# Block 0 of X in four transposing loads of 128 columns, with the Wq quarters between them

## The chip, the cores and the metric

The kernel runs on one core of one Trainium2 chip. The time is device microseconds of one execution; three runs of the kernel before have a median of 168.35 us (168.29 to 169.01). Profiles are taken in an execution of their own; their times count from the first instruction of the span.

The core's engines each run their own instruction queue: PE (matrix products; PEld is its weight load), DVE (VectorE), ACT (ScalarE), POOL (GpSimd) and SP, which only issues DMAs here. They wait for each other on semaphores.

## The reference

Two mixers share the input row-wise through a gate. With S = 2048 rows and D = 512 columns, bfloat16:

```python
x = A_x
g = sigmoid((x * gate_w).sum(-1))
a = sliding_dilated_attention(x, wqkv) @ wo    # 32 heads of 16, 8 keys at distance 0, 2, .., 14
h = layernorm(x)
u = gelu(einsum("bsd,sf->bdf", h, w1) + b1)    # F = 1792
b = (einsum("bdf,fs->bds", u, w2) + b2)        # transposed back to (S, D)
out = g * a + (1 - g) * b
```

The attention first needs q, k and v, three products of x (2048 x 512) with a 512 x 512 part of wqkv each. The change touches the loads for the first of these products.

## The kernel before, in words

The kernel is built from a list of operations, each with its engine, an estimated duration and the buffers it reads and writes. A planner (the class `_Sched`) derives the dependences, orders the operations of every engine greedily by an estimated start and the length of the work that follows, and then plans the waits. For DMAs an estimated landing time can be written by hand (`lands`). Explicit chains at the end fix the order of DVE almost wholly and that of ACT in part; PE's and the rest of ACT's order come out of the planner, so an edited estimate can reorder them.

X is needed in two layouts. Plain X (16 tiles of 128 rows) serves layernorm; XT, its transpose, with 4 tiles of 128 columns (index `dt`) by 2048 rows, is the moving operand of the projections. XT is loaded by transposing DMAs, in four blocks of 512 rows (`sb`). A projection of one block for one group `dl` sums over the four column tiles: four matmuls of 128 x 128 by 512, a weight tile of WQKV each.

In order of time:

- PE first runs warm-up matmuls on constants (L525: nine of 512 columns and one of 256), which are not used.
- Block 0 of q and k goes through eight PSUM banks at once (L609 to L614, matmuls at L593). For q the loop goes over the column tiles outermost: the four groups with column tile 0 (one matmul each), then with tile 1, and so on. Then k, with two column tiles at a time. Here the matmul with column tile `dt` needs that quarter of Wq and, in the kernel before, the whole block 0 of XT.
- The other blocks and v follow (L623 to L632). ACT evicts each group to SBUF (L601 for q, L604 for k and v).
- DVE computes statistics of plain X for layernorm (L548), and products of q with shifted k (L663). PE sums these over a head's columns in two bursts (`qkr_0` and `qkr_1`, L671), which ACT evicts (L701). The second pass of L663 writes over buffers that the first burst reads.
- Softmax on DVE and ACT (L711 to L750), with exponentials at L736; then DVE's weighted sums of v (L770 to L775).
- Meanwhile PE runs the first product of the token mixer (L785), four matmuls per quarter of the rows and 16 per group, each group into one of four banks, evicted by gelu on ACT (L806), and then the second (L835, evicted at L903). At the end come the product with wo (L851), its gated sum on DVE (L872), and the output's DMAs.

The loads issue on SP in the order they are listed in `first_loads` and after it; SP handles one issue at a time, and a wait or a long issue holds everything behind it. The first quarter of Wq issues from ACT's queue (it is named `act` in the list). Issues after the first eight wait for an earlier load (`throttle`: five back in `init_dmas`). L467 is the transposing load of block 0, L460 that of the other blocks, L429 every plain load.

Of the kernel before, what the change touches and what calls it, by code (L numbers as in the profile page):

```python
# [13 lines left out]
D = 512  # L14
# [4 lines left out]
NST = S // 128  # L19
# [314 lines left out]
def bass_gated_mix__sliding_local_dilated__mixer_token_mlp__prompt_kernel(nc, A_x, A_wqkv, A_wo, B_x, B_w1, B_b1, B_w2, B_b2, gate_w, out, dbg=None):  # L334
    with contextlib.ExitStack() as es:
# [3 lines left out]
        sch = _Sched()  # L339

        x2d = A_x[0]
# [7 lines left out]
        XT = view("XT", BF16, [(S, 4), (1, S)])  # L349
# [65 lines left out]
        A = sch.add  # L415
# [12 lines left out]
        def mk_dma(dst, src):  # L428
            return lambda e: e.dma_start(dst, src)  # L429

        init_dmas = []

        def throttle():
            return [init_dmas[-5]] if len(init_dmas) >= 5 else []

        def prev_dma():
            return [init_dmas[-1]] if init_dmas else []

        def ld_x(t0, n, q="sp"):
            ds = sch.dsem("x%d" % t0)  # L440
            op = sch.dma(q, mk_dma(X[:, t0:t0 + n, :], xv[:, t0:t0 + n, :]), n * 128 * D * 2, ds,
                         writes=["x%d" % t for t in range(t0, t0 + n)], deps=throttle() if q == "sp" else [], after=prev_dma() if q == "sp" else [], name="d_x%d" % t0)
            if q == "sp":
                init_dmas.append(op)
            return op

        def ld_w(tn, d0, n, q="sp"):
            ds = sch.dsem("wqkv%d_%d" % (tn, d0))
            op = sch.dma(q, mk_dma(WQKV[:, d0:d0 + n, tn * D:(tn + 1) * D], wqkv_v[:, d0:d0 + n, tn * D:(tn + 1) * D]),
                         n * 128 * D * 2, ds, writes=["wqkv%d_%d" % (tn, dt) for dt in range(d0, d0 + n)],  # L450
                         deps=throttle() if q == "sp" and n == 4 else [], after=prev_dma() if q == "sp" else [],
                         issue=0.65 if n == 4 else 0.45, name="d_wp%d_%d" % (tn, d0))
            if q == "sp":
                init_dmas.append(op)
            return op

        def ld_xt(sb):
            ds = sch.dsem("xt%d" % sb)
            dst = XT[:, :, sb * 512:(sb + 1) * 512]
            op = sch.dma("sp", lambda e: e.dma_start_transpose(dst, x2d[sb * 512:(sb + 1) * 512, :]), 512 * D * 2, ds,  # L460
                         writes=["xt_%d" % t for t in range(4 * sb, 4 * sb + 4)], deps=throttle(), after=prev_dma(), name="d_xt%d" % sb)
            init_dmas.append(op)

        def ld_xt0(s0, s1):
            ds = sch.dsem("xt0_%d" % s0)
            dst = XT[:, :, s0:s1]
            op = sch.dma("sp", lambda e: e.dma_start_transpose(dst, x2d[s0:s1, :]), (s1 - s0) * D * 2, ds, issue=1.25,  # L467
                         writes=["xt_%d" % t for t in range(s0 // 128, s1 // 128)], after=prev_dma(), name="d_xt0_%d" % s0)
            init_dmas.append(op)
            return op  # L470

        first_loads = [ld_w(0, 0, 1, "act"), ld_xt0(0, 512), ld_w(0, 1, 1), ld_w(0, 2, 1), ld_w(0, 3, 1), ld_w(1, 0, 2), ld_w(1, 2, 2),
                       ld_x(0, 2)]
        ld_xt(1)
        first_loads.append(init_dmas[-1])
        for op_, t_ in zip(first_loads, (2.9, 4.9, 5.4, 5.8, 6.2, 7.0, 7.8, 8.6, 11.0)):
            op_.lands = t_
            op_.deps.clear()
        init_dmas[:] = [first_loads[1]] + first_loads[5:]
        ld_x(2, 2)  # L480
        ld_x(4, 4)
        ld_xt(2)
# [6 lines left out]
        def ld_w1(j):  # L489
# [4 lines left out]
            if j < 4:  # L494
# [8 lines left out]
                       writes=["wo"], deps=throttle(), after=prev_dma(), name="d_wo")  # L503
# [4 lines left out]
        for i_, (v_, n_) in enumerate(((B_b1, NFT), (B_b2, NST))):  # L508
            vr = v_.rearrange("(t q j) -> q t j", q=4, j=32)
            for q_ in range(4):  # L510
                sch.dma("sp", mk_dma(psub(BR, 32 * q_, n_, 32 * i_, [(1, 32)]), vr[q_]), n_ * 64, ds_b, reads=["br"],
                        writes=["br_%d_%d" % (i_, q_)], deps=throttle(), after=prev_dma(), name="d_b_%d_%d" % (i_, q_), issue=0.45)
        d_w1.append(ld_w1(3))
        A("dve", lambda e: e.transpose(out=BT, in_=BR), 0.2, reads=["br_%d_%d" % (i_, q_) for i_ in range(2) for q_ in range(4)],
          writes=["btc"], name="t_b")
# [5 lines left out]
        def f_warm(n, w_=D):  # L521
            def fn(e):
                ins = None
                for _ in range(n):
                    ins = e.matmul(ps[:, 7, 0:w_], lhsT=CONE[:, 0:128], rhs=CONE[:, 0:w_], start=True, stop=True)  # L525
                return ins
            return fn

        A("pe", f_warm(9), 3.84, writes=["lg7_0", "lg7_1"], name="warm1", prio=-100)
        last_tx = A("pe", f_warm(1, 256), 0.2, writes=["lg7_0", "lg7_1"], name="warm2", prio=-100)  # L530

        ALLXT = ["xt_%d" % t for t in range(NST)]

        JK = view("OUTS", BF16, [(1, D)], extra=0)
        def cols(v_, lo, n, step=1):
# [9 lines left out]
        for hf in range(2):  # L545
            t0 = 8 * hf
            for t in range(t0, t0 + 8):
                A("dve", (lambda t_: (lambda e: e.bn_stats(out=ST6[:, t_, :], in_=X[:, t_, :])))(t), 0.59,  # L548
                  reads=["x%d" % t], writes=["st6_%d" % t], name="ln1_%d" % t, prio=0)
# [13 lines left out]
              reads=["zc%d" % hf], writes=["sd%d" % hf], name="ln_sqrt%d" % hf, prio=0)  # L563
            A("dve", (lambda t0_: (lambda e: e.reciprocal(out=cols(RSTD, t0_, 8), in_=cols(SD, t0_, 8))))(t0), 0.25,
              reads=["sd%d" % hf], writes=["rstd%d" % hf], name="ln_rstd%d" % hf, prio=0)
# [17 lines left out]
        def main_bank():  # L583
            b = main_idx[0] % 4
            main_idx[0] += 1
            return b
# [22 lines left out]
        for (b0, d0, d1, s0, s1) in ((0, 0, 1, 0, 512), (0, 1, 2, 0, 512), (0, 2, 3, 0, 512), (0, 3, 4, 0, 512), (4, 0, 2, 0, 512), (4, 2, 4, 0, 512)):  # L609
            for b in range(b0, b0 + 4):  # L610
                tn, dl = first[b]
                last_main[0] = A("pe", f_proj(tn, dl, 0, b, d0, d1, s0, s1), 0.216 * (d1 - d0) * (s1 - s0) / 512,
                                 reads=ALLXT[s0 // 128:s1 // 128] + ["wqkv%d_%d" % (tn, dt) for dt in range(d0, d1)],
                                 writes=fbn[b], after=[last_main[0]], name="pf_%s%d_%d_%d" % (tnames[tn], dl, d0, s0))  # L614
        for b, (tn, dl) in enumerate(first):
            A("act", f_evq(tn, dl, 0, b), 0.52, reads=fbn[b] + (["k5pad"] if tn == 1 else []),
              writes=["%s5_%d_0" % (tnames[tn], dl)], name="ev_%s%d_0" % (tnames[tn], dl), prio=0)
# [5 lines left out]
        for dl in range(4):  # L623
            seq_proj += [(2, dl, sb) for sb in range(4)]
        for (tn, dl, sb) in seq_proj:
            xr = ALLXT[4 * sb:4 * sb + 4]
            bank = main_bank()
            last_main[0] = A("pe", f_proj(tn, dl, sb, bank), 0.866,
                             reads=xr + ["wqkv%d_%d" % (tn, dt) for dt in range(4)],
                             writes=["acc%d" % bank], after=[last_main[0]], name="pj_%s%d_%d" % (tnames[tn], dl, sb), prio=0)  # L630
            A("act", f_evq(tn, dl, sb, bank), 0.62, reads=["acc%d" % bank] + (["k5pad"] if tn == 1 else ["v5pad"] if tn == 2 else []),
              writes=["%s5_%d_%d" % (tnames[tn], dl, sb)], name="ev_%s%d_%d" % (tnames[tn], dl, sb), prio=0)  # L632
# [11 lines left out]
                writes=["xa"] + ["wqkv%d_%d" % (tn, dt) for tn in range(3) for dt in range(4)], name="d_xa")  # L644
        for t in range(NST):
# [5 lines left out]
          writes=["th"], name="g_tanh", prio=0)  # L651
        A("dve", lambda e: e.tensor_scalar(out=G, in0=TH, scalar1=0.5, scalar2=0.5, op0=ALU.mult, op1=ALU.add), 0.15,
          reads=["th"], writes=["g"], name="g_g", prio=0)
        A("dve", lambda e: e.tensor_scalar(out=OMG, in0=TH, scalar1=-0.5, scalar2=0.5, op0=ALU.mult, op1=ALU.add), 0.15,
          reads=["th"], writes=["omg"], name="g_omg", prio=0)
        A("dve", lambda e: e.tensor_tensor(out=C2, in0=OMG, in1=B2C, op=ALU.mult), 0.15,
          reads=["omg", "b2c"], writes=["c2"], name="g_c2", prio=0)
# [25 lines left out]
        for wh in range(2):  # L683
# [6 lines left out]
            for (dl, c0, nc_) in pieces:  # L690
# [3 lines left out]
                  reads=["q5_%d_%d" % (dl, sb) for sb in range(c0, c0 + nc_)] +  # L694
                        ["k5_%d_%d" % (dl, sb) for sb in range(max(c0 - 1, 0), c0 + nc_)] + ["k5pad"],
                  writes=wr, name="qkm_%d_%d_%d" % (wh, dl, c0), prio=0)
            rd = sum([pbn(b_) for b_ in bufs], []) + PBX[wh] + ["rp"]
            for wl in range(4):
                qop = A("pe", f_qkr(list(enumerate(bufs)), (wl,)), 0.92, reads=rd, writes=["lg%d_0" % (4 + wl), "lg%d_1" % (4 + wl)],
                        name="qkr_%d_%d" % (wh, wl), prio=-100 + wl, delay=BURST_DELAY)  # L700
                A("act", (lambda wh_, wl_: (lambda e: e.activation(out=ATT[:, :, 4 * wh_ + wl_, :], in_=ps[:, 4 + wl_, :].rearrange("p (h c) -> p h c", h=2), func=AF.Copy)))(wh, wl),  # L701
                  0.55, reads=["lg%d_0" % (4 + wl), "lg%d_1" % (4 + wl)], writes=["lw%d" % (4 * wh + wl)],
                  name="lev_%d_%d" % (wh, wl), prio=0)
# [24 lines left out]
        for hf in range(2):  # L728
# [3 lines left out]
              reads=["outs1"], writes=["lh%d" % hf] + (wall if hf == 0 else []), name="sm_sub%d" % hf, prio=0)  # L732
            if hf == 0:
                A("act", lambda e: e.activation(out=col(SD, 0), in_=col(ZC, 0), func=AF.Exp, scale=0.0), 1.5,
                  reads=["zc0"], writes=["sd0"], name="sm_pre")
            A("act", (lambda hf_, l_: (lambda e: e.activation(out=ATT[:, hf_], in_=l_, func=AF.Exp)))(hf, lgh), 1.95,  # L736
              reads=["lh%d" % hf], writes=["att%d" % hf], name="sm_exp%d" % hf, prio=0)
        for hf in range(2):
# [5 lines left out]
            def f_rcp(e, hf_=hf):  # L744
# [6 lines left out]
              reads=["rs%d" % hf], writes=["att%d" % hf], name="sm_nrm%d" % hf, prio=0)  # L751
# [4 lines left out]
        for u in range(8):  # L756
            c, hf = u // 2, u % 2
            ds_at = sch.dsem("atx%d" % u)
            for a_ in range(4):
                dst = bass.AP(ATX.tensor, ATX.offset + a_ * pst + u * NW * HC, [[4 * pst, 32], [1, NW * HC]])  # L760
                sch.dma("act", mk_dma(dst, psub(ATT, 32 * c, 32, hf * NW * HC, [(1, NW * HC)])), 32 * NW * HC * 2, ds_at, issue=0.62,
                        reads=["att%d" % hf], writes=["atx_%d_%d" % (u, a_)], deps=pb_readers, name="d_atx_%d_%d" % (u, a_))
        USEQ = [0, 2, 1, 3, 4, 6, 5, 7]
        for k_, u in enumerate(USEQ):
# [6 lines left out]
              reads=v_res + ["atx_%d_%d" % (u, a_) for a_ in range(4)], writes=[pn] + [qk_res, k_all][k_ % 2], name="avm_%d" % u)  # L771
            for (nm, n_, du) in (("ava", 4, 2.25), ("avb", 2, 1.2)):
                A("dve", (lambda pv_, n__: (lambda e: e.tensor_tensor(out=pv_[:, 0:n__], in0=pv_[:, 0:n__], in1=pv_[:, n__:2 * n__], op=ALU.add)))(pv, n_),  # L773
                  du, writes=[pn], name="%s_%d" % (nm, u))
# [27 lines left out]
        for ft in range(NFT):  # L802
# [4 lines left out]
                                                                bias=col(B1C, ft_))))(ft, bank), 0.72,  # L807
              reads=["acc%d" % bank, "b1c"], writes=["ut%d" % ft] + ALLXT,
              name="gel_%d" % ft, prio=0)
# [84 lines left out]
        for i in range(NST):  # L894
# [4 lines left out]
            elif i > 1:  # L899
# [5 lines left out]
              reads=["acc%d" % bank, "omg", "c2"], writes=["t1_%d" % i, "x%d" % i],  # L905
              name="t1_%d" % i, prio=0)
# [119 lines left out]
```

## Time and profile before

| | us |
|---|---|
| median of three runs | 168.35 |
| span of the profiled execution, first to last instruction | 167.55 |
| PE busy | 164.4 |
| DVE busy | 150.9 |
| ACT busy | 74.6 |

The profiled execution's own time is its span; the runs are timed without a profile and include what lies around the span.

Landing times of the first loads in the profiled execution, from issue to landing:

| load | issued | landed |
|---|---|---|
| Wq quarter 0 (ACT's queue) | 0.80 | 3.02 |
| XT block 0 (L467) | 0.80 | 5.14 |
| Wq quarters 1, 2, 3 | 2.25, 3.05, 3.51 | 5.52, 5.87, 6.21 |
| Wk, two halves | 3.99, 4.46 | 7.02, 8.61 |
| plain X tiles 0 and 1 | 4.98 | 9.50 |
| XT block 1 (L460) | 5.49 | 11.45 |
| plain X tiles 2 and 3 | 9.33 | 12.35 |

How to read the lines below. In a timeline a line is: start, duration, engine (a q behind it marks the engine's instruction queue, as for an issued DMA), source line, operation, written and read names, count, and in brackets the idle time before it with what ended it. In a windows answer a line is: the stretch, its length, the busy time of each engine with the number of instructions that touch the stretch, the granted clock, the DMA engines' busy share, and GB/s.

### The profile page before, as it was taken

How to read it: one execution, taken by the hardware profiler on the slowest of the kernel's cores; microseconds unless marked ns; L12 is line 12 of the kernel's file. 1: busy time of each engine (PE TensorE's matmuls, PEld its weight loads, DVE VectorE, ACT ScalarE, POOL GpSimd, SP SyncE). 2: the span in 40 equal slices, each digit the busy share in tenths (PEclk: the TensorE clock that was granted, in tenths of full speed). 3: DMA queues.
4: the chain of work that ended last, by engine and by line, in shares of the span. 5: the costliest groups of instructions: out<-in, count | busy, mean ns of one | idle time of the engine just before them, and what ended most of it. 6: DMA issues, size and time to landing. Idle time of an engine off the chain costs nothing.

```text
span 167.5 us, 2143 instructions
## 1 busy us (share of the span) xinstructions
PE 164.4 (98%) x858; PEld 77.8 (46%) x858; DVE 150.9 (90%) x153; ACT 74.6 (45%) x115; POOL 0.7 (0%) x8
## 2 busy tenths in 40 slices
PE   8999999999999999999999999999999999999994
PEld 2355555554454444444444444444444444444463
DVE  0035999999899999999999999999999999999896
ACT  3067688889899818793122131131231321310100
POOL 1000000000000000000000000000000000000000
DMA  6999999969003946996789915462672580000454
GB/s 151 280 249 276 310 319 291 302 199 263 0 0 83 323 116 173 304 290 159 172 230 337 342 49 137 117 189 68 182 215 82 142 223 0 0 0 0 157 192 157
DMA packets 47609, 29.64 MB, mean 177 GB/s; under 512 B 9840, under 2 KB 46448, under 8 KB 47600
## 3 DMA queue, kind: packets, MB, share of 16 engines
q1 hardware_dynamic: 45632, 24.98, 54.5%
q10 hardware_dynamic: 1968, 4.52, 9.8%
q8 instruction: 7, 0.11, 0.3%
q14 instruction: 2, 0.02, 0.0%
HBM read 21.11 MB, written 2.10 MB: 139 GB/s over the span
## 4 chain that ended last, share of the span: by engine, by line
PE 94%; DMA 3%; DVE 2%; issue 0%
PE ps L785 29%; PE ps L835 29%; PE ps L593 25%; PE ps L851 6%; PE ps L671 4%; DMA arena<-in_A_x_dram 3%; DVE arena L872 2%
## 5 line engine op out<-in xcount | busy, mean ns | idle before, releaser
L785 PE MATMUL ps<-arena 128*128 128x512 bf16 x224 | 48.7, 380 | 0.0
L835 PE MATMUL ps<-arena 128*128 128x512 bf16 x224 | 48.7, 380 | 0.0
L593 PE MATMUL ps<-arena 128*128 128x512 bf16 x192 | 42.4, 384 | 0.2 <-DMA arena<-in_A_x_dram 0.2
L663 DVE TENSOR_TENSOR arena<-arena 128x4096 bf16<-128x4096 bf16 (+1 forms) x12 | 35.5, 2997 | 2.1 <-ACT arena L604 1.7
L770 DVE TENSOR_TENSOR arena<-arena 128x8192 bf16<-128x8192 bf16 x8 | 35.0, 4420 | 0.0
L835 PEld LDWEIGHTS ps<-arena 128*128 128x128 bf16 x224 | 21.9, 98 | 26.4
L785 PEld LDWEIGHTS ps<-arena 128*128 128x128 bf16 x224 | 21.8, 98 | 26.6 <-ACT arena L701 0.4
L593 PEld LDWEIGHTS ps<-arena 128*128 128x128 bf16 x192 | 21.7, 114 | 21.1 <-issue 1.7
L903 ACT ACTIVATE arena<-ps,arena 128x512 bf16<-128x512 f32 x16 | 12.4, 778 | 39.4 <-PE ps L835 39.4
L773 DVE TENSOR_TENSOR arena<-arena 128x4096 bf16<-128x4096 bf16 (+1 forms) x16 | 27.0, 1753 | 0.0
L604 ACT ACTIVATE arena<-ps 128x512 bf16<-128x512 f32 x32 | 18.5, 596 | 4.5 <-PE ps L593 4.5
L806 ACT ACTIVATE arena<-ps,arena 128x512 bf16<-128x512 f32 x14 | 9.6, 687 | 22.2 <-PE ps L785 16.7
L548 DVE BATCH_NORM_STATS2 arena<-arena 128x6 f32<-128x512 bf16 x16 | 10.0, 681 | 9.6 <-DMA arena<-in_A_x_dram 9.6
L851 PE MATMUL ps<-arena 128*128 128x512 bf16 (+1 forms) x80 | 14.2, 337 | 0.0
L601 ACT ACTIVATE arena<-ps 128x512 bf16<-128x512 f32 x16 | 9.0, 596 | 8.1 <-PE ps L593 8.0
L872 DVE SCALAR_TENSOR_TENSOR arena<-ps,arena 128x512 bf16<-128x512 f32 (+1 forms) x20 | 11.5, 639 | 0.9 <-PE ps L851 0.7
L572 ACT ACTIVATE arena<-arena 128x512 bf16<-128x512 bf16 x16 | 12.2, 804 | 0.0
L851 PEld LDWEIGHTS ps<-arena 128*128 128x128 bf16 x80 | 7.8, 98 | 6.2
L647 DVE SCALAR_TENSOR_TENSOR arena<-arena 128x512 bf16<-128x512 bf16 x16 | 10.1, 687 | 0.0
L717 DVE TENSOR_TENSOR arena<-arena 128x512 bf16<-128x512 bf16 (+4 forms) x11 | 7.3, 667 | 0.6 <-ACT arena L736 0.2
L671 PE MATMUL ps<-arena 128*32 128x512 bf16 x128 | 7.3, 380 | 0.0
L701 ACT ACTIVATE arena<-ps 128x512 bf16<-128x512 f32 x8 | 4.7, 591 | 4.6 <-PE ps L671 4.6
(38 smaller groups left out, 39.8 us busy)
## 6 DMA issues: line engine op xcount, KB each, us to landing
arena<-in_B_w_dram SPq DMA_DIRECT2D x7, 1024.0 KB, 8.3
arena<-in_B_w_dram SPq DMA_DIRECT2D x8, 896.0 KB, 5.2
arena<-arena ACTq DMA_DIRECT2D x32, 128.0 KB, 2.9
arena<-in_A_x_dram SPq DMA_DIRECT2D x4, 512.0 KB, 5.5
out_dram<-arena SPq DMA_DIRECT2D x14, 128.0 KB, 1.7
arena<-in_A_x_dram SPq DMA_DIRECT2D x1, 1536.0 KB, 7.9
arena<-in_A_wqkv_dram SPq DMA_DIRECT2D x2, 256.0 KB, 3.6
arena<-in_A_x_dram SPq DMA_DIRECT2D x2, 256.0 KB, 3.8
```

Source lines behind the costliest of these rows:

```text
L572: A("act", (lambda t_: (lambda e: e.activation(out=X[:, t_, :], in_=X[:, t_, :], func=AF.Identity, scale=col(RSTD, t_), bias=col(NMR, t_)) ...
L593: ins = e.matmul(ps[:, bank, s0:s1], lhsT=lhsT, rhs=XT[:, dt, sb * 512 + s0:sb * 512 + s1], start=(dt == 0 and s0 == 0), stop=(dt == 3))
L604: return lambda e: e.activation(out=dst, in_=ps[:, bank, :], func=AF.Copy)
L663: return lambda e: e.tensor_tensor(out=PBL[buf][:, :, 512 * c0:512 * (c0 + nc_)], in0=in0, in1=in1, op=ALU.mult)
L671: ins = e.matmul(ps[32 * c:32 * c + 32, 4 + wl, :], lhsT=RP, rhs=PBL[buf][:, wl, c * 512:(c + 1) * 512], start=(dl == 0), stop=(dl == 3), ...
L770: A("dve", (lambda o_, i0, i1: (lambda e: e.tensor_tensor(out=o_, in0=i0, in1=i1, op=ALU.mult)))(pv, in0, in1), 4.4, reads=v_res + ["atx_% ...
L773: A("dve", (lambda pv_, n__: (lambda e: e.tensor_tensor(out=pv_[:, 0:n__], in0=pv_[:, 0:n__], in1=pv_[:, n__:2 * n__], op=ALU.add)))(pv, n ...
L785: ins = e.matmul(ps[:, bank, :], lhsT=W1W[:, slot, st, 128 * e_:128 * e_ + 128], rhs=X[:, st, :], start=(st == 0), stop=(st == NST - 1))
L835: ins = e.matmul(ps[:, bank, :], lhsT=W2S[slot][:, ft, 128 * e_:128 * e_ + 128], rhs=UT[:, ft, :], start=(ft == 0), stop=(ft == NFT - 1))
L851: ins = e.matmul(ps[:, bank, 0:c1 - c0], lhsT=OT[:, t, 128 * i:128 * i + 128], rhs=WO[:, t, c0:c1], start=(t == 0), stop=(t == 3))
L872: A("dve", (lambda i_, b_, c0_, c1_: (lambda e: e.scalar_tensor_tensor(out=T1[:, i_, c0_:c1_], in0=ps[:, b_, 0:c1_ - c0_], scalar=col(G, i ...
L903: A("act", (lambda i_, bank_: (lambda e: e.activation(out=T1[:, i_, :], in_=ps[:, bank_, :], func=AF.Identity, scale=col(OMG, i_), bias=co ...
```

## The change

The one transposing load of block 0 (512 rows by 512 columns) becomes four, each of 512 rows by 128 columns, all on SP. They alternate with the Wq quarters: column tile 0, Wq 1, column tile 1, Wq 2, column tile 2, Wq 3, column tile 3, then the two halves of Wk. Each has its own buffer name (`xt0_0` to `xt0_3`), and a q matmul of block 0 waits for its own column tile only. Plain X tiles 0 and 1 move from ahead of XT block 1 to behind it. The warm-up goes from nine matmuls of 512 columns to five (and one of 256, as before). The hand-written landing times are new.

```diff
-        def ld_xt0(s0, s1):
-            ds = sch.dsem("xt0_%d" % s0)
-            dst = XT[:, :, s0:s1]
-            op = sch.dma("sp", lambda e: e.dma_start_transpose(dst, x2d[s0:s1, :]), (s1 - s0) * D * 2, ds, issue=1.25,
-                         writes=["xt_%d" % t for t in range(s0 // 128, s1 // 128)], after=prev_dma(), name="d_xt0_%d" % s0)
+        def ld_xt0(d):
+            ds = sch.dsem("xt0_%d" % d)
+            dst = XT[:, d:d + 1, 0:512]
+            op = sch.dma("sp", lambda e: e.dma_start_transpose(dst, x2d[0:512, 128 * d:128 * d + 128]), 512 * 128 * 2, ds, issue=0.4,
+                         writes=["xt0_%d" % d], after=prev_dma(), name="d_xt0_%d" % d)
...
-        first_loads = [ld_w(0, 0, 1, "act"), ld_xt0(0, 512), ld_w(0, 1, 1), ld_w(0, 2, 1), ld_w(0, 3, 1), ld_w(1, 0, 2), ld_w(1, 2, 2),
-                       ld_x(0, 2)]
+        first_loads = [ld_w(0, 0, 1, "act"), ld_xt0(0)]
+        for d_ in range(1, 4):
+            first_loads += [ld_w(0, d_, 1), ld_xt0(d_)]
+        first_loads += [ld_w(1, 0, 2), ld_w(1, 2, 2)]
         ld_xt(1)
         first_loads.append(init_dmas[-1])
-        for op_, t_ in zip(first_loads, (2.9, 4.9, 5.4, 5.8, 6.2, 7.0, 7.8, 8.6, 11.0)):
+        first_loads.append(ld_x(0, 2))
+        for op_, t_ in zip(first_loads, (2.9, 3.1, 3.6, 4.0, 4.5, 4.9, 5.4, 5.8, 6.7, 7.6, 10.4, 11.2)):
             op_.lands = t_
             op_.deps.clear()
-        init_dmas[:] = [first_loads[1]] + first_loads[5:]
+        init_dmas[:] = first_loads[7:]
...
-        A("pe", f_warm(9), 3.84, writes=["lg7_0", "lg7_1"], name="warm1", prio=-100)
+        A("pe", f_warm(5), 2.13, writes=["lg7_0", "lg7_1"], name="warm1", prio=-100)
...
+        def xt_of(sb, d0=0, d1=4):
+            return XT0[d0:d1] if sb == 0 else ["xt_%d" % t for t in range(4 * sb, 4 * sb + 4)]
...
-                                 reads=ALLXT[s0 // 128:s1 // 128] + ["wqkv%d_%d" % (tn, dt) for dt in range(d0, d1)],
+                                 reads=xt_of(0, d0, d1) + ["wqkv%d_%d" % (tn, dt) for dt in range(d0, d1)],
```

In the compiled order PE keeps all its instructions, but each burst of L671 comes four matmuls later among the others: 156 matmuls of the projections stand before the first burst instead of 152, and 52 instead of 48 matmuls of L785 stand before the second. On ACT some evictions move by a place against the layernorm operations; among them, the eviction of k for group 0, block 3 now stands before the square root (L561) and the table load in front of it. DVE's order is as before.

More of the change, by code (lines that the diff above doesn't have):

```diff
@@ L527, in f_warm @@
             return fn
-        A("pe", f_warm(9), 3.84, writes=["lg7_0", "lg7_1"], name="warm1", prio=-100)
+        A("pe", f_warm(5), 2.13, writes=["lg7_0", "lg7_1"], name="warm1", prio=-100)
         last_tx = A("pe", f_warm(1, 256), 0.2, writes=["lg7_0", "lg7_1"], name="warm2", prio=-100)
-        ALLXT = ["xt_%d" % t for t in range(NST)]
+        XT0 = ["xt0_%d" % d for d in range(4)]
+        ALLXT = XT0 + ["xt_%d" % t for t in range(4, NST)]
+        def xt_of(sb, d0=0, d1=4):
+            return XT0[d0:d1] if sb == 0 else ["xt_%d" % t for t in range(4 * sb, 4 * sb + 4)]
         JK = view("OUTS", BF16, [(1, D)], extra=0)
@@ L625, in bass_gated_mix__sliding_local_dilated__mixer_token_mlp__prompt_kernel @@
         for (tn, dl, sb) in seq_proj:
-            xr = ALLXT[4 * sb:4 * sb + 4]
+            xr = xt_of(sb)
             bank = main_bank()
```

## The prediction

> **What bounds the kernel now.** I read the page first, then the timeline of the first 14 us, then stretches of it by windows, then the places where VectorE and ScalarE meet TensorE again. From the page and the timeline:
>
> ```profile
> PE 164.4 (98%) x858; PEld 77.8 (46%) x858; DVE 150.9 (90%) x153; ACT 74.6 (45%) x115; POOL 0.7 (0%) x8
> PE 94%; DMA 3%; DVE 2%; issue 0%
> ...
> 0.80 0.38 ACTq L429 DMA_DIRECT2D arena<-in_A_wqkv_dram  x1
> 0.80 1.39 SPq L467 DMA_TRANSPOSE arena<-in_A_x_dram  x1
> 0.84 4.21 PE L525 MATMUL ps<-const-bfloat16-1.0 128*128 128x512 bf16 x10 [0.84 <-PEq L1011]
> 2.25 2.68 SPq L429 DMA_DIRECT2D arena<-in_A_wqkv_dram  x5
> 5.27 9.00 PE L593 MATMUL ps<-arena 128*128 128x512 bf16 x38 [0.23 <-DMA arena<-in_A_x_dram]
> ```
>
> PE runs from 0.84 us to the tail with a single gap, 0.23 us. So whatever moves the first real matmul (5.27) moves the end, unless a new wait appears. The 5.27 is set by the transposing DMA on SP: issued at 0.80, it holds SP for 1.39 and lands 4.34 later (5.14); the matmul starts 0.13 after that. Until then PE runs ten warm-up matmuls that compute nothing.
>
> Next, the clock and the bytes, in two windows answers:
>
> ```profile
> 5.20:6.60 1.40, 1.33 (x4) 1.00 1.10 303
> 6.70:12.70 6.00, 6.00 (x30) 1.00 1.05 256
> ```
> ```profile
> 0.80:1.75 0.95, 0.91 (x3) 0.39 (x4) 0.28 (x1) 0.54 (x1) 0.54 (x4) 1.00 0.00 0
> 1.75:2.25 0.50, 0.50 (x3) 0.20 (x2) 0.00 (x0) 0.50 (x1) 0.00 (x0) 1.00 0.63 170
> 2.25:4.50 2.25, 2.25 (x7) 0.76 (x5) 0.00 (x0) 0.24 (x1) 0.00 (x0) 1.00 1.25 289
> ```
>
> The first answer counts L593 alone: 4 matmuls begin in 1.40 us, then 30 touch 6.00 us. A 512-column matmul costs 0.427 us up to about 6.6 us (the warm-ups: 4.21 us for nine and a half) and 0.216 after it, although the clock column says 1.00 throughout. So real work done before 6.6 us saves only half its place: a start earlier by t gains 0.495 t (1 - 0.216/0.427). In the second answer no byte moves before 1.75, 0.95 us after both first DMAs were issued. Up to 2.25 there are 85 KB, less than the 131 KB quarter of Wq on ACT's queue, so the transpose moves nothing before about 2.25, just after its hold ended at 2.19. The hold is then mostly a start-up; afterwards bytes flow at 289 GB/s, 0.45 us for 128 KB.
>
> **What the change does, with its costs.** Call the four transposes T0 to T3, the Wq quarters w0 to w3, the Wk halves ka and kb.
>
> *Removed:* four warm-ups, 4 x 0.427 = 1.71 us. They now end at 0.84 + 5 x 0.427 + 0.21 = 3.19. T0 carries a quarter of the data: it lands at the whole's 4.34 less three quarters of 2.25 (1.69), 2.65 after issue, at 3.45, so matmuls can start at 3.58. That alone would gain (5.27 - 3.58) x 0.495 = 0.84 us.
>
> *Added on SP:* three more transposes, each in front of a load that PE needs. What one of 128 columns holds the queue for the trace doesn't show. Bounds: 0.35 (a quarter of 1.39, all of it by size) and 1.39 (none of it). I take 0.95 as free of size, the delay which both kinds of DMA show before the first byte, plus a quarter of the remaining 0.44: 1.06, nearer to the upper row for the reason above. A plain DMA right behind a transpose: 0.75 for w1, 0.58 and 0.58 for the X loads at 9.33 and 15.87; mean 0.64, bounds 0.42 (the shortest plain row) and 0.75. With gaps of 0.06 and 0.05 a pair is 1.12 + 0.69 = 1.81. So T3 issues at 0.80 + 3 x 1.81 = 6.23 and ka at 0.80 + 4 x 1.12 + 3 x 0.69 = 7.35; before, ka issued at 3.99.
>
> [...]
>
> *On the path:* T1 lands by 2.61 + 2.65 = 5.26, where PE is done with T0's four slow matmuls (5.29). T2 lands at 7.07, a few tenths late; T3 at 8.88, so its four end at 9.01 + 0.86 = 9.87. ka: w0 took 2.22 us for 128 KB, the second 128 KB add 0.45, so it lands at 7.35 + 2.67 = 10.02 and PE starts on it at 10.15. Before it started there at 9.36. **The early start is won and lost again: PE is 0.79 us late.** kb (0.9 later, 10.92) is needed at 10.15 + 8 x 0.216 = 11.88. Block 1's transpose, behind kb with 512 KB (1.8 to 2.25 us), lands by 13.2, needed at 13.6. Both hidden; without that cover block 1 would cost its lateness one for one.
>
> *Plain X behind block 1* is hidden too. The first X load lands near 14.1 instead of 9.5, the second near 15.0 instead of 12.35; DVE's four L548 (1.29 a pair) end near 16.3, and L663 waits for L604's k eviction anyway, 15.34 + 0.79 = 16.13. DVE starts up to 0.9 late. It has room:
>
> ```profile
> 15.37 4.50 DVE L663 TENSOR_TENSOR arena<-arena 128x4096 bf16<-128x4096 bf16 x2 [1.71 <-ACT arena L604]
> 42.50 4.43 DVE L663 TENSOR_TENSOR arena<-arena 128x8192 bf16<-128x8192 bf16 x1 [0.42 <-PE ps L671]
> 73.91 2.25 ACT L806 ACTIVATE arena<-ps,arena 128x512 bf16<-128x512 f32 x3
> 157.65 8.29 DVE L872 SCALAR_TENSOR_TENSOR arena<-ps,arena 128x512 bf16<-128x512 f32 x15 [0.72 <-PE ps L851]
> ```
>
> At 42.50 DVE waits for PE's L671, which ends at 0.79 + 0.86 later: the compiled order puts one projection group (four matmuls, 0.86) ahead of each L671 burst. Total PE work is unchanged, but DVE runs 1.65 late from there. That reaches PE at one place. The third gelu group's bank is freed by the first of the three L806 at 73.91, done at 74.60; PE wants it at 65.06 + 48 x 0.216 = 75.43. With DVE 1.65 and PE 0.79 late, 76.25 + 0.04 against 76.22: 0.07 us more. At the end DVE has slack: its twenty L872 need about 11.0 us of work (twelve of 0.66, eight of 0.39), so 153.55 + 1.65 + 11.0 = 166.2, before PE's last result allows 165.94 + 0.86 = 166.80. The ScalarE reordering (an eviction ahead of a table load of 1.28) can cost DVE 0.5 near 25 us, under the same cover.
>
> **Sum:** +0.79 + 0.07 = +0.86. The profiled execution has a span of 167.55, so 168.41; the median of the runs is 168.35, 0.80 more, for what lies around the span: **169.2 us**. Its own range: short bounds (0.95 and 0.45 per hold) put ka at 6.34, PE 0.22 early, 168.2; long ones (1.39 and 0.75) put it at 9.00, PE 2.44 late, 170.9.
>
> **Rivals.**
>
> *The hold goes by size (0.35).* [...] Against: the bytes began when the hold ended. ka issues at 0.80 + 4 x 0.41 + 2.07 = 4.51 and lands at 7.18, in time; T0 is there at 2.41, and start is at the warm-ups' end, 3.20. Gain 2.07 x 0.495 = 1.02, less the 0.07 at the gelu bank: 167.4. It decides while ka lands before 9.23, which is a hold under 0.87. Chance 0.20.
>
> *The clock stays at half longer.* PE now has gaps in the stretch that ended in the faster clock; before there was one of 0.23. If gaps delay it through ka's eight matmuls: 8 x 0.211 = 1.69, plus T3's group ending at 10.72 instead of 10.15: 171.4. Against: PE is still busy most of 3.6 to 6.6. Chance 0.12. [...]
>
> *Early start and late weights cancel*, with waits elsewhere unchanged: 168.3, a pair of about 1.6. Chance 0.10.
>
> **How the numbers follow.** My case has 0.58. From no change a measurement of this kernel can tell about 0.5%, 0.84 us: below 167.51, above 169.19. Faster: three quarters of the first rival, 0.15. Slower: the clock rival and 0.40 of my case, 0.52. The rest, 0.33, lies within. The range 167.5 to 171.0 leaves out about half of the first rival and two thirds of the second, under 0.2.
>
> **What would show it.** Holds of the three inner L467 near 1.1 and ka issued near 7.3 confirm the mechanism; holds under 0.6 with the first k matmul before 9.0 refute it. First real matmul near 3.6, gaps in PE before the third and fourth quarter and before ka; matmul starts 0.43 apart only until about 6.6; DVE idle before the second L663 pass over 1 us. I am wrong if the queue accepts these transposes without holding, or if PE shows no gap after 3.6.

## The result, and the profile after

The changed kernel takes 171.11 us (median of 4 runs, 170.78 to 171.53), the kernel before beside it 168.59 (168.29 to 169.01, 4 runs): ratio of the runs 1.0156, 95% interval 1.0128 to 1.0184 (the two medians alone give 1.0149). It is slower, by 2.5 us; forecast were 169.2 us and a range that ended at 171.0.

Two lines of the changed kernel's page, the engines' busy time and the chain that ended last, and then its timeline:

```profile
PE 162.1 (96%) x840; PEld 76.7 (45%) x854; DVE 150.7 (89%) x153; ACT 74.7 (44%) x115; POOL 0.7 (0%) x8
...
PE 90%; SPq 4%; DVE 2%; DMA 2%; issue 1%
```
```profile
0.80 1.23 SPq L467 DMA_TRANSPOSE arena<-in_A_x_dram  x1
0.84 2.50 PE L528 MATMUL ps<-const-bfloat16-1.0 128*128 128x512 bf16 x6 [0.84 <-PEq L1018]
...
2.70 1.14 SPq L467 DMA_TRANSPOSE arena<-in_A_x_dram  x1
3.75 1.27 PE L600 MATMUL ps<-arena 128*128 128x512 bf16 x4 [0.41 <-DMA arena<-in_A_x_dram]
...
4.50 1.12 SPq L467 DMA_TRANSPOSE arena<-in_A_x_dram  x1
5.59 1.03 PE L600 MATMUL ps<-arena 128*128 128x512 bf16 x4 [0.57 <-DMA arena<-in_A_x_dram]
...
6.29 1.12 SPq L467 DMA_TRANSPOSE arena<-in_A_x_dram  x1
7.46 1.09 SPq L429 DMA_DIRECT2D arena<-in_A_wqkv_dram  x2
7.63 1.03 PE L600 MATMUL ps<-arena 128*128 128x512 bf16 x4 [1.02 <-DMA arena<-in_A_x_dram]
...
9.37 1.03 PE L600 MATMUL ps<-arena 128*128 128x512 bf16 x4 [0.71 <-DMA arena<-in_A_x_dram]
...
11.16 3.21 PE L600 MATMUL ps<-arena 128*128 128x512 bf16 x14 [0.77 <-DMA arena<-in_A_wqkv_dram]
```

The lines of this kernel are numbered 7 higher from the projections on (L600 is the former L593). The single gap of 0.23 has become five, 3.48 us together, one in front of each column tile and one in front of the k projection. SP's queue has entered the chain. (14 of the 854 matmuls have no record in this trace, so PE's busy time reads a little low.) The four transposes hold SP for 1.12 to 1.23 us each, and the first Wk half (ka) is issued at 7.46, where it was 3.99. The k projection begins at 11.16, where it was 9.36: 1.80 us late. The span is 169.49, where it was 167.55: 1.94 more.

The clock and the bytes, as before in windows, first of L600 alone (length, TensorE's busy time, granted clock, DMA share, GB/s), then of all engines:

```profile
5.20:6.60 1.40, 1.01 (x4) 1.00 0.85 159
6.70:12.70 6.00, 3.59 (x15) 1.00 0.93 206
```
```profile
2.25:4.50 2.25, 1.84 (x7) 0.51 (x5) 0.00 (x0) 0.25 (x1) 0.00 (x0) 1.00 0.72 180
4.50:9.40 4.90, 2.61 (x12) 0.84 (x11) 0.00 (x0) 0.00 (x0) 0.00 (x0) 1.00 0.72 141
```

In 5.20 to 6.60 four matmuls need only 1.01 us, so the clock was already up (matmul starts are 0.216 apart from 4.42). In 6.70 to 12.70, 15 matmuls are busy for 3.59 us, where 30 filled it. The bytes flow at 141 to 180 GB/s, where the single transpose ran at 289, and the DMA engines' busy share is 0.72, where it was 1.25. That fits an SP that now hands them too little at a time.

And where VectorE and ScalarE meet TensorE:

```profile
17.20 4.50 DVE L670 TENSOR_TENSOR arena<-arena 128x4096 bf16<-128x4096 bf16 x2
45.19 4.42 DVE L670 TENSOR_TENSOR arena<-arena 128x8192 bf16<-128x8192 bf16 x1 [0.82 <-PE ps L678]
76.61 2.25 ACT L813 ACTIVATE arena<-ps,arena 128x512 bf16<-128x512 f32 x3
156.24 11.63 DVE L879 SCALAR_TENSOR_TENSOR arena<-ps,arena 128x512 bf16<-128x512 f32 x20
```

Four places that were at 15.37, 42.50, 73.91 and 153.55 are 1.83, 2.69, 2.70 and 2.69 later. The 0.82 of idle time in front of 45.19 is a wait for TensorE: VectorE had room left there.

### The profile page after: what moved, and what is told of

Its sections match the earlier page's. It is cut to its first block, busy times and chain, and to the rows that moved or that the text cites. A ratio compares the mean times of both kernels' runs of the same rounds, so it can differ in the third digit from the quotient of the medians.

```text
span 169.5 us, 2127 instructions
## 1 busy us (share of the span) xinstructions
PE 162.1 (96%) x840; PEld 76.7 (45%) x854; DVE 150.7 (89%) x153; ACT 74.7 (44%) x115; POOL 0.7 (0%) x8
## 4 chain that ended last, share of the span: by engine, by line
PE 90%; SPq 4%; DVE 2%; DMA 2%; issue 1%
PE ps L792 28%; PE ps L842 28%; PE ps L600 22%; PE ps L858 6%; PE ps L678 4%; SPq L467 3%; DVE arena L879 2%; DMA arena<-in_A_wqkv_dram 2%; SPq L429 1%
## 5 line engine op out<-in xcount | busy, mean ns | idle before, releaser
L600 PE MATMUL ps<-arena 128*128 128x512 bf16 x188 | 42.3, 381 | 3.8 <-DMA arena<-in_A_x_dram 2.7
L600 PEld LDWEIGHTS ps<-arena 128*128 128x128 bf16 x192 | 21.3, 114 | 25.1 <-DMA arena<-in_A_wqkv_dram 6.0
L555 DVE BATCH_NORM_STATS2 arena<-arena 128x6 f32<-128x512 bf16 x16 | 9.9, 679 | 13.3 <-DMA arena<-in_A_x_dram 13.3
L813 ACT ACTIVATE arena<-ps,arena 128x512 bf16<-128x512 f32 x14 | 9.6, 687 | 21.1 <-PE ps L792 15.6
```

The source lines that it names most:

```text
L600: ins = e.matmul(ps[:, bank, s0:s1], lhsT=lhsT, rhs=XT[:, dt, sb * 512 + s0:sb * 512 + s1], start=(dt == 0 and s0 == 0), stop=(dt == 3))
```

## The experiments

One number orders them all. The table has the start of the k projection (the 17th matmul after the warm-ups, by TensorE's records of the profiled execution), the span of that execution, the difference, the median time, and the ratio to the kernel before with its 95% interval.

| kernel | k starts | span | span - k start | time | ratio |
|---|---|---|---|---|---|
| one_transpose | 8.70 | 166.89 | 158.19 | 168.15 | 0.9998 (0.9986 to 1.0011) |
| halves | 9.12 | 167.51 | 158.39 | 169.57 | 1.0064 (1.0038 to 1.0091) |
| before_again | 9.25 | 167.44 | 158.19 | 168.71 | one run |
| before, as first shown | 9.36 | 167.55 | 158.19 | 168.35 | 1 |
| halves_w10 | 9.37 | 167.58 | 158.21 | 168.81 | 1.0036 (1.0013 to 1.0058) |
| halves_sp | 9.87 | 168.08 | 158.21 | 169.32 | 1.0047 (1.0032 to 1.0063) |
| k_act_w9 | 10.80 | 169.02 | 158.22 | 170.33 | 1.0103 (1.0073 to 1.0132) |
| warm9 | 10.90 | 169.20 | 158.30 | 170.74 | 1.0152 (1.0137 to 1.0166) |
| the changed kernel | 11.16 | 169.49 | 158.33 | 171.11 | 1.0156 (1.0128 to 1.0184) |
| k_act | 11.26 | 169.59 | 158.33 | 170.69 | 1.0131 (1.0110 to 1.0151) |
| ka_alone | 11.64 | 170.34 | 158.70 | 171.59 | one run |
| five | 11.67 | 170.83 | 159.16 | 172.10 | 1.0218 (1.0193 to 1.0243) |
| plain_act | 13.47 | 171.91 | 158.44 | 171.17 | 1.0211 (1.0169 to 1.0253) |

In eleven of the thirteen the span is the start of the k projection plus 158.2 to 158.4, whatever the loads do. (Between the first, third and fourth row that start differs by when the clock rose: matmul starts are 0.216 apart from 5.46, 6.44 and 6.77.) Two kernels stand off: in `five` four more matmuls ran at half clock behind that start (4 x 0.211 = 0.84), and in `ka_alone` TensorE waits once more, for a later transposing load of X (the matmul at 23.25 starts 0.57 after the one before it instead of 0.22). A median differs from the profiled execution where executions spread: `plain_act` was profiled in one of 173.17.

### The split undone, the rest kept: one_transpose

```diff
-            dst = XT[:, d:d + 1, 0:512]
-            op = sch.dma("sp", lambda e: e.dma_start_transpose(dst, x2d[0:512, 128 * d:128 * d + 128]), 512 * 128 * 2, ds, issue=0.4,
+            dst = XT[:, :, 0:512]
+            op = sch.dma("sp", lambda e: e.dma_start_transpose(dst, x2d[0:512, :]), 512 * D * 2, ds, issue=1.25,
...
-        A("pe", f_warm(5), 2.13, writes=["lg7_0", "lg7_1"], name="warm1", prio=-100)
+        A("pe", f_warm(9), 3.84, writes=["lg7_0", "lg7_1"], name="warm1", prio=-100)
```

> The changed kernel with the split undone: one transpose of 512 columns, then the Wq quarters and Wk halves as before, nine warm-ups; plain X stays behind block 1. Queue theory: the time of the kernel before within 0.3 us, since the reordered X loads are hidden. Rival (late plain X costs): 0.5 us or more slower than before, with DVE starting its first product later than 15.4 and PE waiting for its bursts.

Measured: 168.15 us (11 runs), ratio 0.9998. Its timeline:

```profile
0.80 1.39 SPq L467 DMA_TRANSPOSE arena<-in_A_x_dram  x1
...
2.24 2.58 SPq L429 DMA_DIRECT2D arena<-in_A_wqkv_dram  x5
4.87 2.93 SPq L460 DMA_TRANSPOSE arena<-in_A_x_dram  x1
5.16 9.10 PE L597 MATMUL ps<-arena 128*128 128x512 bf16 x40
7.84 1.61 SPq L429 DMA_DIRECT2D arena<-in_A_x_dram  x3
```

Plain X stands behind block 1 here too (7.84, behind the L460 of 4.87), and the timeline shows no gap of TensorE in front of 5.16. The warm-ups and the loads that later issues wait for are those of before as well; the warm-ups are taken up alone in the next experiment. So plain X costs nothing in its new place, and the split with what it pushes back is the whole loss.

### The warm-ups given back: warm9

```diff
-        A("pe", f_warm(5), 2.13, writes=["lg7_0", "lg7_1"], name="warm1", prio=-100)
+        A("pe", f_warm(9), 3.84, writes=["lg7_0", "lg7_1"], name="warm1", prio=-100)
```

> The changed kernel with nine warm-up matmuls again. Queue theory: PE waits for loads anyway, the first quarter's matmuls move from 3.75 to about 5.05 into time that was idle, the first k matmul stays near 11.2, and the time is that of the changed kernel within 0.3 us. Rival (the shorter warm-up holds the clock at half or costs otherwise): 0.8 us or more faster than the changed kernel.

Measured: 170.74 us, ratio 1.0152; from the changed kernel's 1.0156 it can't be told. The clock was up before the first real matmul (at 4.21, four in 1.02 us), and the end still hangs on ka, issued at 7.45 and landed at 10.85:

```profile
10.90 3.43 PE L600 MATMUL ps<-arena 128*128 128x512 bf16 x15 [0.89 <-DMA arena<-in_A_wqkv_dram]
```

The four warm-ups that were taken out are not the cause, nor is the clock in this kernel. PE's compiled order here was that of before, so the order isn't either.

### How long ka takes: ka_alone

The first Wk half waits until the last column tile has landed, so that it runs alone.

```diff
             op_.deps.clear()
+        first_loads[8].deps.add(first_loads[7])
```

> The changed kernel in which the first Wk half waits until the fourth transpose has landed, so that it starts on an empty queue. If a plain load behind a transpose is slowed by it, the 256 KB land 2.6 to 2.7 us after issue here, against 3.66 (3.40 with nine warm-ups) in the changed kernel. Rival (256 KB on a drained queue take that long by themselves): 3.3 us or more here too. The end moves later by what the first k matmul does, to about 12.0 or 12.7.

The last line of the DMA view, for a window that holds this issue alone (number, KB, us from issue to landing), of the changed kernel and then of `ka_alone`:

```profile
arena<-in_A_wqkv_dram SPq DMA_DIRECT2D x1, 256.0 KB, 3.7
```
```profile
arena<-in_A_wqkv_dram SPq DMA_DIRECT2D x1, 256.0 KB, 2.7
```

The same 256 KB take 3.66 us right behind a transpose and 2.68 alone (issued 8.92, landed 11.60). It was issued 1.46 later and landed 0.48 later. So one microsecond of ka's lateness is not its later issue but its flight behind what is still under way, the transpose last.

The packets in the traces (1 KB each in a plain load, 256 bytes in a transpose) divide this microsecond. Behind the transpose ka's issue holds SP for 0.58 instead of 0.39, and its first packet starts 1.24 after the issue instead of 1.03; that is 0.2. The other 0.8 comes after the first packet. From there to the landing it takes 2.42 us in the changed kernel and 2.17 in `warm9`, where the transpose ahead lands only after that packet has started (9.23 against 8.70, and 8.84 against 8.68). It takes 1.65 alone, and 1.67 in the next kernel, `five`, where the transpose ahead has landed before it (9.77 against 9.95). So ka was slow where the transpose ahead of it was unfinished. What in the DMA engines does this was not tried.

### One transpose more: five

The last column tile is loaded in two transposes of 256 rows each (`ld_xt0` gets the rows as arguments).

```diff
-        for d_ in range(1, 4):
+        for d_ in range(1, 3):
             first_loads += [ld_w(0, d_, 1), ld_xt0(d_)]
+        first_loads += [ld_w(0, 3, 1), ld_xt0(3, 0, 256), ld_xt0(3, 256, 512, "b")]
```

> The changed kernel with column tile 3 in two transposes of 256 rows, back to back: one hold more, the same bytes. Queue theory: every transpose holds SP 1.1 us whatever its size, so the first Wk half issues about 1.17 us later (8.6 against 7.46), the first k matmul starts about 1.1 us later (12.2 to 12.4), and the time is 1.0 to 1.2 us above the changed kernel's ratio to before: about 1.022 to 1.023 of it. Rival (it is the bytes that are slow): the split costs less than 0.3 us.

Measured: 172.10 us, ratio 1.0218, against 1.0156 of the changed kernel. Its timeline at the fifth transpose, and windows of its L602, the projections:

```profile
6.29 2.39 SPq L467 DMA_TRANSPOSE arena<-in_A_x_dram  x2
7.34 1.03 PE L602 MATMUL ps<-arena 128*128 128x512 bf16 x4 [0.27 <-DMA arena<-in_A_x_dram]
8.72 1.09 SPq L429 DMA_DIRECT2D arena<-in_A_wqkv_dram  x2
...
9.90 4.29 PE L602 MATMUL ps<-arena 128*128 128x512 bf16 x11 [1.53 <-DMA arena<-in_A_x_dram]
```
```profile
7.30:8.40 1.10, 1.03 (x4) 1.00 0.47 123
9.90:13.30 3.40, 3.40 (x8) 0.51 1.00 236
13.40:16.00 2.60, 2.60 (x14) 1.00 1.08 289
```

Two transposes of 64 KB hold SP for 2.39 together, no less than two of 128 KB: here a hold is paid per transpose, not per byte. ka is issued 1.26 later than in the changed kernel. The size of the loss is near what was expected, but part of it came another way: ka flew for 2.90 only and k started 0.51 later, and then the clock was at half again from 9.90 to 13.3, with 0.51 granted (eight matmuls in 3.40 us), right behind a gap of 1.53.

### The weights on ScalarE's queue: plain_act, k_act, k_act_w9

`k_act` issues the two Wk halves on ACT's queue behind Wq 0, `plain_act` all plain weights, `k_act_w9` is `k_act` with nine warm-ups. The diff of `k_act`, and the line that `plain_act` changes beside it:

```diff
-        first_loads += [ld_w(1, 0, 2), ld_w(1, 2, 2)]
+        first_loads += [ld_w(1, 0, 2, "act"), ld_w(1, 2, 2, "act")]
...
+        act_loads = [o for o in first_loads if o.eng == "act"]
+        for a_, b_ in zip(act_loads, act_loads[1:]):
+            b_.order.add(a_)
```
```diff
-            first_loads += [ld_w(0, d_, 1), ld_xt0(d_)]
+            first_loads += [ld_w(0, d_, 1, "act"), ld_xt0(d_)]
```

> The changed kernel with the two halves of Wk issued from ACT's queue behind the first Wq quarter; SP keeps the four transposes and the three other Wq quarters. Queue theory (each small transpose holds SP about 1.1 us, and what is issued behind it starts that much later): the transposes land as in the changed kernel (the fourth near 9.2), Wk is there before them, so the first k matmul starts near 10.2 instead of 11.16 and the end comes about 0.9 us earlier than the changed kernel's, still some 1.3 us or more behind the kernel before. Rival (the bytes of small transfers are slow whatever the queue): the Wk bytes, sent earlier, push the transposes back, the fourth lands at 9.8 or later, and less than 0.4 us is gained.

> The changed kernel with all five plain weight loads (three Wq quarters, two Wk halves) on ACT's queue; SP issues the four transposes back to back, then block 1. Queue theory: inner transposes issue every 1.2 us, at about 0.8, 2.0, 3.2, 4.3; the fourth lands near 7.3, the first k matmul starts near 8.3 against 9.36 before, and the kernel is 0.5 to 1.0 us faster than before. Rival (slow bytes): each quarter takes about 1.2 us of data time and the weights share the engines, so the fourth lands at 8.5 to 9, k starts at 9.4 or later, and the kernel is no faster than before.

> The run with Wk on ACT's queue, with nine warm-ups in place of five, so that PE has no gap of 2.3 us before the first real matmul. If that gap kept the clock at half (matmul starts 0.43 apart up to 10.5 us in that run): the starts go to 0.22 apart by about 7, the first k matmul starts near 9.8 to 10, and the time is about 169.0 to 169.4 beside 168.2 before. Rival (the warm-up doesn't matter, as in the run with nine warm-ups and all loads on SP): again 170.5 or more.

None gets back to the kernel before, and none does what its theory said: in `k_act` the fourth transpose landed at 8.80, earlier than in the changed kernel (9.23), and k still started at 11.26 and not near 10.2; in `plain_act` it landed at 10.17, later than its rival had it; `k_act_w9` missed the start of 9.8 to 10. The view of the L467 alone in `plain_act` (holds in ns, then us to landing):

```profile
L467 SPq DMA_TRANSPOSE arena<-in_A_x_dram x4: 1217/1248/1261, 0.8 to 4.7; - x4
...
DMA to landing us min/median/max: 4.4/5.3/6.6
```

The holds stay at 1.2 us with nothing between them, but a landing takes 4.4 to 6.6 us, where the changed kernel's take 2.8 to 3.0: the first tile, issued at the same 0.80, lands at 5.24 for 3.61. `k_act` shows the same with nothing changed on SP up to there, only the two Wk halves more on ACT's queue: its first tile lands at 5.08. So with the weights' bytes on ACT's queue the first tile lands 1.47 to 1.63 us later. That these bytes take the DMA engines from it is the author's estimate: from 3.70 to 5.20, while the tile was on its way in `k_act`, the engines there moved 317 GB/s at a busy share of 1.10, and 145 GB/s at 0.60 in the changed kernel.

The late first tile opens a gap, and there the clock stays down. `k_act`, windows of its L603:

```profile
5.20:6.60 1.40, 1.39 (x4) 1.00 1.26 203
6.70:10.60 3.90, 3.90 (x10) 1.00 0.80 158
10.80:14.20 3.40, 3.40 (x17) 1.00 0.84 227
```

TensorE waits from 3.34 to 5.21, then ten matmuls fill 3.90 us although the column of the clock says 1.00; only from 10.61 do they run at 0.216. ka is there in time, and the k projection still starts at 11.26. With nine warm-ups (`k_act_w9`) there is no such gap and the clock is up from about 6.2, so this part goes with the gap; but then tile 2 lands at 7.55 and tile 3 at 9.80 (8.80 in `k_act`, issued at the same time within 0.03), TensorE waits for both (0.25 and 1.23 us), and k starts at 10.80, only 0.46 earlier than in `k_act`.

### Fewer holds: halves, halves_w10, halves_sp

Two transposes of 256 columns. In `halves` they stand back to back with Wq 0 and 1 on ACT's queue and seven warm-ups; `halves_w10` has ten; `halves_sp` has Wq 1 on SP between them, and seven. First `halves` against the changed kernel, then `halves_sp` against `halves`:

```diff
-            dst = XT[:, d:d + 1, 0:512]
+            dst = XT[:, d:d + 2, 0:512]
...
+        first_loads = [ld_w(0, 0, 1, "act"), ld_w(0, 1, 1, "act"), ld_xt0(0), ld_xt0(2), ld_w(0, 2, 1), ld_w(0, 3, 1), ld_w(1, 0, 2), ld_w(1, 2, 2)]
```
```diff
-        first_loads = [ld_w(0, 0, 1, "act"), ld_w(0, 1, 1, "act"), ld_xt0(0), ld_xt0(2), ld_w(0, 2, 1), ld_w(0, 3, 1), ld_w(1, 0, 2), ld_w(1, 2, 2)]
+        first_loads = [ld_w(0, 0, 1, "act"), ld_xt0(0), ld_w(0, 1, 1), ld_xt0(2), ld_w(0, 2, 1), ld_w(0, 3, 1), ld_w(1, 0, 2), ld_w(1, 2, 2)]
```

> Two transposes of 256 columns, back to back at the head of SP; Wq quarters 0 and 1 on ACT's queue at the start, Wq 2 and 3 and Wk behind the transposes on SP; seven warm-ups. Queue theory: two holds, so the second transpose issues near 2.1 and SP is free for plain loads near 3.3; the transposes land near 4.2 and 5.5, the first Wk half near 7.3, PE starts real work near 4.4 and k at 7.9 to 8.7, and the kernel is 0.3 to 0.9 us faster than before. Rival (any split loses more by shared bytes than it gains): the first transpose lands at 5 or later and the time is that of before or longer.

> The kernel 'halves' (two transposes of 256 columns back to back, Wq 0 and 1 on ACT's queue) with ten warm-ups of 512 columns for seven, which fill the 1.48 us in which PE waited for the first transpose. Theory: the spread of 'halves' (168.42 to 170.85, while its loads should land the same each time) is the clock, which in some executions stays at half behind that gap; then without the gap the spread closes to that of the kernel before (168.1 to 168.9) and the median falls to 168.2 to 168.6 (ratio 0.999 to 1.001). Rival: the loads themselves land late in some executions, since ACT's and SP's bytes run side by side; then warm-ups change nothing, the median stays near 169.6 (ratio 1.005 to 1.009) and the spread above 2 us.

> Two transposes of 256 columns, all on SP except Wq 0: first half of X, Wq 1, second half, Wq 2 and 3, Wk; seven warm-ups. Only one hold stands in front of the first landing, and no other queue's bytes beside it but Wq 0. Theory (one transpose more costs SP about 1.25 us, a landing on a quiet queue comes 2.8 to 3.3 after issue): the first half lands at 3.9 to 4.2, where the warm-ups end (4.04); the second is issued near 2.7 and lands by 6.0 to 6.5, before its first matmul at 7.4; the first Wk half is issued near 5.2 and lands by 8.5, before 9.0: no gap over 0.3, the start is won by 1.1 to 1.3 us at half weight, 0.5 to 0.6, so a span near 166.4 and a ratio of 0.996 to 0.998. Rival (a plain load behind a transpose lands 3.4 to 3.7 after issue, so Wq 1 and Wq 2 come late and the clock is held by the gaps): gaps of 0.5 us or more before Wq 1's or Wq 2's matmuls, ratio 1.003 to 1.01.

`halves` 169.57, `halves_w10` 168.81, `halves_sp` 169.32: all between the two kernels, none faster than before. In `halves` the first half of X lands at 5.53, no earlier than the whole of it did (5.14), as its rival had it: Wq 1 on the other queue and the second transpose right behind are under way beside it. In `halves_sp`, where Wq 1 stands between the two on SP, it lands at 4.37. In `halves_w10` the warm-ups leave no gap in front of the first real matmul, and the median falls by 0.76, which is not as far as its theory had it; but the spread stays at 2.06 us (168.22 to 170.28). A gap in front of Wq 2 took the place of the first one. The timeline of `halves_w10` and its DMA view for that issue:

```profile
7.64 8.58 PE L600 MATMUL ps<-arena 128*128 128x512 bf16 x39 [0.61 <-DMA arena<-in_A_wqkv_dram]
```
```profile
arena<-in_A_wqkv_dram SPq DMA_DIRECT2D x1, 128.0 KB, 4.0
```

The same load at the same place took 3.18 us in `halves` (issued 3.49) and 4.00 here (issued 3.51). So the loads vary. The clock's part is not shown: in the profiled execution of `halves`, one of its faster ones (168.78), matmul starts are 0.216 apart from the first real one on, in spite of the gap of 1.48. How much of the spread each makes stays open. `halves_sp` shows its rival's picture:

```profile
0.80 1.32 SPq L467 DMA_TRANSPOSE arena<-in_A_x_dram  x1
...
2.79 1.23 SPq L467 DMA_TRANSPOSE arena<-in_A_x_dram  x1
4.06 2.05 SPq L429 DMA_DIRECT2D arena<-in_A_wqkv_dram  x4
4.51 2.52 PE L600 MATMUL ps<-arena 128*128 128x512 bf16 x8 [0.31 <-DMA arena<-in_A_x_dram]
...
8.15 8.15 PE L600 MATMUL ps<-arena 128*128 128x512 bf16 x37 [1.12 <-DMA arena<-in_A_wqkv_dram]
```

The start is won, 4.51 for 5.27, and lost again in one gap of 1.12 in front of Wq 2, which landed at 8.01, 3.95 after issue, right behind a transpose. In the traces a load lands in 16 steps of its semaphore; 15 of Wq 2's had come by 7.07, and the last came 0.94 later. In `halves_w10` 14 had come by 6.35, and the last at 7.51. Why one part stays behind was not tried.

### What lies around the span: before_again

The kernel before, unchanged.

> The kernel before, profiled once more, to see what the prediction's base was worth. Theory: the 0.80 us between the profiled span before (167.55) and the median time (168.35) was too little, because that execution's clock rose late (6.77); the time of a run is its own span plus about 1.27, as in the changed kernel (170.78 against 169.5) and in the kernel with one transpose (168.15 against 166.9). Expected: a span of 166.8 to 167.2, matmul starts 0.216 apart from before 6 us on, and a time 1.2 to 1.3 above the span. Rival (0.80 is what lies around the span, and the changed kernel adds 0.45 there): the listed time is 0.75 to 0.85 above the span, whatever the clock does.

A profiled execution has a listed time of its own, so both numbers can be had from one execution. Here the listed time is 168.71 and the span 167.44: 1.27 around it, not 0.80, so the rival falls. The theory's span of 166.8 to 167.2 was missed too, since the clock rose late again here (0.216 apart from 6.44). In the other executions of this study whose span is listed the difference is 1.2 to 1.4.

## Why the prediction was wrong, step by step

**Right: the hold.** Inner transposes at 1.06 and plain DMAs behind them at 0.64, a pair of 1.81; measured 1.12 to 1.14, 0.55 to 0.58 and 1.80. The first term was 0.07 too low and the second 0.07 too high, so it is luck that the pair came out within 0.01, while its make-up is right. T3 issued at 6.29 (6.23 forecast) and ka at 7.46 (7.35). The rival that the hold goes by size needed less than 0.87 and falls, and `five` refutes it for 64 KB as well.

**Wrong: the flight of ka.** The step "it lands at 7.35 + 2.67 = 10.02 and PE starts on it at 10.15" gave ka the time of a load on an empty queue. That term is right for an empty queue (2.68 in `ka_alone`), but this load stands behind a transpose and took 3.66. PE started on it at 11.16, so it was 1.80 late instead of 0.79. This is the larger part of the miss: of the 1.01, 0.99 is the flight and 0.11 the later issue, less 0.09 because the matmul followed the landing sooner than forecast. The trace of before had the sign of it: w1, 128 KB right behind the transpose, took 3.27 (2.25 to 5.52), where w0 of the same size took 2.22, and ka itself took 3.03 there (3.99 to 7.02). I used w0's row.

**Wrong: what lies around the span.** 0.80 was one execution's span taken from the median of other runs; the two belong to different executions. Within one execution it is 1.29 (170.78 less 169.49) and 1.27 in `before_again`. The profiled execution of before, whose clock rose only at 6.77, was thus about 0.5 us longer than the median one. The step that made "168.41" into "169.2" was short by 0.49.

The miss of 1.91 (171.11 less 169.2) is then 1.01 from the start of the k projection, 0.49 from around the span, 0.33 from the median against the profiled execution (171.11 less 170.78), and 0.07 inside the span. The range took its upper end from longer holds alone and had no term for a longer flight.

**The start.** T0 landed at 3.61 and matmuls began at 3.75 (3.45 and 3.58 forecast). The gain was real and worth nothing, as the forecast had it: in front of the k projection TensorE waits anyway. T1 to T3 landed 0.19 to 0.43 later than forecast, since they flew for 2.75 to 3.00 instead of 2.65; that was not on the path either, because ka landed later still.

**The clock.** The sign "matmul starts 0.43 apart only until about 6.6" missed: they are 0.216 apart from 4.42 on, which gains nothing while TensorE waits for loads. The rival in which the clock stays at half did not happen in the changed kernel, but elsewhere it was at half behind a gap: in `k_act` until 10.61 (ten matmuls in 3.90 us) and in `five` from 9.90 to 13.3 (0.51 granted). Here no gap was longer than 1.02 us; that this is why it stayed out is not shown.

**Hidden edits.** Plain X behind block 1 costs nothing: `one_transpose` keeps it at a ratio of 0.9998, and in the changed kernel VectorE still idles 0.82 at 45.19 (forecast as over 1 us). VectorE's lateness there was forecast as PE's plus 0.86; 1.80 + 0.86 = 2.66, measured 2.69. The gelu bank was forecast at 0.07; the span's growth beyond the start of the k projection is 0.14 (1.94 less 1.80). Of this 0.09 arises at that bank: the weight load at 77.35 waits for the first of the three L813 (76.61 to 77.30), and the matmul starts 0.30 after the one before it instead of 0.22.

**Early start and late weights cancel** needed a pair of 1.6 and falls with the pair of 1.80. Its idea survives in the halves, which have fewer holds and come within 0.4 to 0.6% of the kernel before.

## What to carry to other kernels

Count transposing DMAs by number, not by bytes: here each of the first ones held the queue for 1.1 to 1.3 us between 64 and 256 KB, and the plain load right behind it took 0.2 to 1.8 us longer to land than one on an empty queue, so in this kernel the split could pay only if nothing urgent stood behind it. Look for the first matmul group that the split does not feed (here k) and forecast its start; here the span followed it within 0.3 us in eleven of thirteen kernels. Take the time around a span from an execution that has both numbers, never from one execution's span and another's time.

## What the runs showed of the hardware

- **The hold of the first transposes hardly depended on size.** 64 KB: 1.10 and 1.24; 128 KB: 1.12 to 1.26; 256 KB: 1.23 to 1.32; 512 KB: 1.39 as the first load of the queue. Block 1, also 512 KB but behind all of these loads, held SP for 2.42 (`k_act`) to 3.80 us (before), so size is not all that counted; what it waited for was not tried.
- **A plain load right behind a transpose was late, and by a varying amount.** 128 KB took 2.54 us (Wq 3 of `k_act`) to 4.00 (`halves_w10`) where 2.22 is a first load's time; 256 KB took 2.90 (`five`) to 3.66, and 2.68 alone. Plain loads further behind were late too (Wq 3 of `halves`: 4.04), so the transpose is what was ahead here, and need not be the only thing that delayed a load.
- **The clock came down again behind a gap of 1.53 us.** In `five` it was up at 7.34 (four matmuls in 1.03 us) and at half from 9.90 (0.51 granted), behind 1.53 us of idle TensorE; the page's row of the clock shows it in its third slice:

```profile
PEclk9969999999999999999999999999999999999999
```

In `ka_alone` a gap of 1.58 left it up (1.00 granted, 11 matmuls in 2.57 us behind it), so the length of a gap didn't decide alone. The record of the clock in `five` has it full from 6.58 to 9.99 and half from 9.99 to 13.40, 3.41 us each, and TensorE was busy for 1.61 of the first stretch. What made it fall is not shown.
- **The clock column missed the start.** It says 1.00 in `k_act` while ten matmuls take 3.90 us (starts 0.43 apart, and 0.216 from 10.61 on); the spacing of the matmuls was the surer sign.
